# First k rows on ScalarE's DMA queue, v rows ahead of the weights, and the first masks as a bias product on TensorE

## The chip, the cores and the metric

The kernel runs on one core of one Trainium2 chip. The metric is the device time of one execution in microseconds (us). A profiled execution also has a span, from the first instruction to the last, which is about 1.7 us shorter than its time. Every time is a median of 3 to 6 runs, and the interval of its ratio to the kernel before is given with it.

The engines are called by their short names in the profile: PE is TensorE's matmuls, PEld its weight loads, DVE VectorE, ACT ScalarE, POOL GpSimd and SP SyncE.

## The reference

Sliding-window attention with four sink keys feeds a small mixture of experts in which every expert sees every token. B, H, S, D = 4, 8, 768, 64; window 128; 3072 tokens of 512 features; 4 experts with a hidden size of 1024.

```python
scores = scale * np.matmul(q, k.transpose(0, 1, 3, 2))
keep   = is_sink | in_window          # key < 4, or 0 <= query - key < 128
scores = np.where(keep, scores, -1e9)
a      = softmax(scores)
x      = np.matmul(a, v)              # heads put side by side: 3072 x 512
p      = domain_probs / (domain_probs.sum(-1, keepdims=True) + 1e-09)
for e in range(4):
    out += p[:, e:e+1] * (np.maximum(x @ w1[e], 0) @ w2[e])
```

## The kernel before

The sequence of each of the four batches is cut into three groups of 256 tokens. Attention of the first groups of batch 0 comes first; expert products start as soon as the first rows of x exist and from then on hide the attention of everything that follows. So the start is the only place where TensorE has too little to do. It is filled with idle products (matmuls of zeros, put there to keep the granted clock up; it is 1.00 in the windows below).

The order in which instructions are put on each engine is made at build time by a small model: `t[...]` are modelled engine times, `landed[...]` modelled arrivals of loads, and `later(engine, ready, slack, run)` puts an instruction in when the model thinks it is ready. Constants such as 4700.0 below are such modelled nanoseconds. They change the order of instructions and nothing else.

Loads go out on two kinds of queues. `nc.sync` and `nc.scalar` are plain queues, issued from SP and ACT. `nc.gpsimd` is the software queue: POOL spends about 0.9 us on each issue, one load after the other.

```python
def load_first():                       # q and k rows of the first group, two halves
    for half in range(2):
        for name, src in (("q", q), ("k", k)):
            nc.sync.dma_start(out=raw[name][:, half], in_=...)     # cut
        landed["first", half] = ((4700.0, 4700.0), (7000.0, 7900.0))[half]
        t["sp"] += 1060

# ... cut: the program's order at the start
load_v(0, (0, 1))                       # POOL: v0, v1
# POOL: two affine selects make the identity
for tb in (2, 3):
    load_nat(0, tb)                     # POOL: q, k rows of the second group (4 loads, tile qkn)
load_w1(0, 2)                           # POOL: first expert's w1 in two halves
# DVE: identity, then six instructions that make mask0 and mask1
cast_first(0)                           # ACT casts k, DVE casts q (first half)
# POOL: two affine selects make the selector sel2
cast_first(1)
load_v(0, (2, 3))                       # POOL: v2, v3
load_w2(0)

def scores(b, hp, g):                   # one pair of heads, one group
    # ... TensorE: 6 products into sps ; ACT: exp into a
    # batch 0: DVE multiplies each half of a by mask0 or mask1
```

The softmax here doesn't subtract the row's maximum and nothing guards it: scores larger than these inputs give would overflow.

Of the kernel before, what the change touches and what calls it, by code (L numbers as in the profile page):

```python
# [16 lines left out]
def kernel(  # L17
# [12 lines left out]
    nc = tc.nc  # L30
# [29 lines left out]
    NGATE = 5  # L60
    START = {0: 1, 1: 2}
    ONACT = 1
    FAST = tuple(START)
    UNITS = ("P1", "P5", "P6", "P2", "P7", "P3", "P4")
    DX = D + 1
# [1 line left out]



    t = {"pe": 1200.0, "act": 0.0, "dve": 0.0, "pool": 420.0, "sp": 800.0, "sw": 4700.0, "hw": 0.0}  # L70
    ring, whole = [0.0] * 6, [False] * 6
    WARM = 6600.0
    FLIP, LATE = 300, 2500
# [40 lines left out]
    def later(engine, ready, slack, run):  # L114

        pend.append((ready, ready + slack, engine, run))
# [89 lines left out]
    def load_first():  # L206

        raw = {name: mo.tile([P, 2, 4, 2 * D], FP32, name=f"{name}raw", tag=f"wide{i}", bufs=1) for i, name in enumerate("qk")}
        for half in range(2):
            hs = slice(4 * half, 4 * half + 4)  # L210
            for name, src in (("q", q), ("k", k)):
                x = raw[name][:, half]
                nc.sync.dma_start(
                    out=x, in_=src[0, hs, 0:G, :].rearrange("h (p t) d -> p h (t d)", t=2),
                )
                nat[0, half, name, "raw"] = x
            landed["first", half] = ((4700.0, 4700.0), (7000.0, 7900.0))[half]
            t["sp"] += 1060

    def copy(engine, out, in_):  # L220
        (nc.scalar.copy if engine == "act" else nc.vector.tensor_copy)(out=out, in_=in_)
# [168 lines left out]

    held = consts.tile([P, 2], BF16, name="held")
    nc.vector.memset(identf, 1.0)
    zeros = wpool.tile([P, 2 * G], BF16, name="zeros", tag=f"wf_{E - 2}")
    nc.vector.memset(zeros, 0.0)
    vsf = consts.tile([P, B, DX], FP32, name="vsf")
    nc.vector.memset(vsf, 0.0)
# [1 line left out]
    for h in range(H):  # L398
# [1 line left out]
        nc.sync.dma_start(  # L400
            out=vsf[r:r + NSINK, :, 0:D], in_=v[:, h, 0:NSINK, :].rearrange("b j d -> j b d"),
        )
    load_v(0, (0, 1))
    ident = consts.tile([P, P], BF16, name="ident")
    for sgn in (1, -1):
        nc.gpsimd.affine_select(
# [1 line left out]
            base=0, pattern=[[sgn, P]], channel_multiplier=-sgn,  # L408
        )
        pool(0, fixed=320)  # L410
    for tb in (2, 3):
        load_nat(0, tb)
    load_w1(0, 2)

    for x in vx:
        nc.vector.memset(x[:, :, D:DX], 1.0)
    nc.vector.tensor_copy(out=ident, in_=identf)
    mask0 = consts.tile([P, 3 * P], BF16, name="mask0")
    mask1 = consts.tile([P, 4 * P], BF16, name="mask1")
    nc.vector.tensor_tensor_scan(mask0[:, 0:P], ident, ident, 0.0, ALU.add, ALU.max)  # L420
    own = mask0[:, 0:P]
    prev = mask0[:, P:2 * P]
    nc.vector.tensor_scalar(out=prev, in0=own, scalar1=-1.0, scalar2=1.0, op0=ALU.mult, op1=ALU.add)
    for i, x in enumerate((prev, own)):
        nc.vector.tensor_copy(
            out=mask1.rearrange("p (n c q) -> p n c q", n=2, c=2)[:, :, i], in_=x[:, None, :].to_broadcast([P, 2, P]),
        )
    nc.vector.tensor_copy(out=mask0[:, 2 * P:3 * P], in_=own)
    nc.vector.memset(mask0[0:NSINK, 0:2 * P], 1.0)
    t["dve"] = 4600.0  # L430
    cast_first(0)
    flush(4700.0)

    sel2 = consts.tile([P, NHP, 2, DX], BF16, name="sel2")
    vsd = {}
    half = consts.tile([P, 2], BF16, name="half")
    ksd = [consts.tile([P, NHP, 32], BF16, name=f"ksd{i}") for i in range(2)]

    nc.vector.memset(sel2, 1.0)
    for base, sgn in ((0, 1), (NSINK - 1, -1)):  # L440
        nc.gpsimd.affine_select(
            out=sel2, in_=sel2, compare_op=ALU.is_ge, fill=0.0, base=base,
            pattern=[[-32 * sgn, NHP], [-NSINK * sgn, 2], [0, DX]], channel_multiplier=sgn,
        )
        pool(0, fixed=700)
    nc.vector.memset(half, 0.0)
    for ph in range(2):
        nc.vector.memset(half[64 * ph:64 * ph + 64, ph:ph + 1], 1.0)
    for x in ksd:
        nc.vector.memset(x, 0.0)  # L450
    t["dve"] += 900.0
    cast_first(1)
    load_v(0, (2, 3))
    load_w2(0)

    acc = [psum.tile([P, 2 * G], FP32, name=f"acc{i}", tag=f"o{i}", bufs=1) for i in range(2)]

# [104 lines left out]
    def scores(b, hp, g):  # L562
        T = qkT[b]
        w = sum(x[2] for x in GROUPS[g]) * P
        ready = scores_ready(b, hp, g)
        slots, sps = [], []
        for ph in range(2):
            i = pick()
            slots.append(i)
            sps.append(bank(i, [P, 2 * G], FP32, "sps"))  # L570
            ring[i] = 1e12
        c = 0
        for (kb, qb, nq) in GROUPS[g]:
            for ph in range(2):
                pr = slice(64 * ph, 64 * ph + 64)
                nc.tensor.matmul(  # L576
                    sps[ph][:, c:c + nq * P],
                    lhsT=T[pr, 1, hp, kb * P:(kb + 1) * P],
                    rhs=T[pr, 0, hp, qb * P:(qb + nq) * P],
                    start=True, stop=True,  # L580
                )
            c += nq * P
        scored_at[b] = done = pe(w, ready, n=6, switch=2)
        a = sb.tile([P, 2, w], BF16, name="aT", tag="aT", bufs=4)
        m = mask0 if g == 0 else mask1

        def masked(at):
            aT_at[b, hp, g] = at

        if b == 0:  # L590
            part = join(2, masked)
        else:
            def mask_both(at):
                def run(engine):
                    nc.vector.tensor_mul(a, a, m[:, None, :].to_broadcast([P, 2, w]))  # L595
                    masked(dve(2 * w, rate=1.92))
                later("dve", at, 1500, run)
            part = join(2, mask_both)
        for ph in range(2):
            def run(engine, ph=ph):  # L600
                nc.scalar.activation(out=a[:, ph], in_=sps[ph][:, 0:w], func=AF.Exp, scale=scale)  # L601
                at = act(w)
                take(slots[ph], at)
                if b:
                    part(at)
                    return

                def mask_one(engine):
                    nc.vector.tensor_mul(a[:, ph], a[:, ph], m)
                    part(dve(w, rate=1.92))  # L610
                later("dve", at, 300, mask_one)
            later("act", done, 300 + 10 * ph, run)
        aTs[b, hp, g] = a
# [101 lines left out]
    class Attention:  # L715
# [23 lines left out]
        def options(self):  # L739

            if self.valued:
                yield turn_ready(*self.valued[0]), "turn"
            if self.scored and len(self.valued) < 3:
                yield values_ready(*self.scored[0]), "values"
            if self.todo:
                kind, b, x, y = self.todo[0]
                if kind == "scores":
                    if len(self.scored) < 3:
                        yield scores_ready(b, x, y), "todo"
                elif kind == "keys":  # L750
                    yield max(turned(b, 0)), "todo"
                elif kind == "sinks":
                    yield max([free_at(), keys_at.get(b, 1e12)] + turned(b, x)), "todo"
            if self.flips:
                yield self.flip_ready() + (FLIP if self.b == 0 and self.flips[0][2] else 0), "flip"
# [620 lines left out]
```

## Time and profile before

| | before |
|---|---|
| time, median of 3 runs | 379.82 us (379.15 to 380.06) |
| PE busy, share of the span | 97% |
| idle products, all before 18 us | 7.42 us |
| first transpose (its weight load) starts | 6.51 us |
| scores of the second group start | 16.49 us |
| first expert product starts | 17.80 us |

The page's first part gives busy time and share of the span for each engine:

```profile
PE 367.0 (97%) x3954; PEld 298.7 (79%) x3954; DVE 271.8 (72%) x619; ACT 146.6 (39%) x383; POOL 71.6 (19%) x91
```

TensorE is full, but part of that is filler. The windows view of the idle products alone (window, its length, PE busy with the number of products, PEld busy, granted clock, DMA share, GB/s) shows where:

```profile
0.00:10.00 10.00, 5.66 (x20) 2.25 (x20) 1.00 1.23 162
10.00:14.00 4.00, 0.83 (x3) 0.29 (x3) 1.00 1.80 183
14.00:18.00 4.00, 0.93 (x7) 0.64 (x7) 1.00 1.50 195
...
```

The timeline of the start (start, busy time, engine, line, operation, out<-in, count, and in brackets the idle time before with what ended it) shows why the first transpose comes at 6.51 us:

```profile
4.72 0.62 ACT L221 CAST qkn<-kraw 128x512 bf16<-128x512 f32 x1 [2.64 <-DMA kraw<-in_k_dram]
...
4.96 0.80 DVE L425 COPY mask<-mask 128x256 bf16<-128x256 bf16 x2
...
6.10 0.35 DVE L221 CAST qkn<-qraw 128x512 bf16<-128x512 f32 x1
...
6.51 0.62 PE L479 MATMUL tr<-ident,qkn 128*128 128x128 bf16 x8 [0.87 <-DVE qkn L221]
```

The k rows are in at 4.7 us and cast at once. The q rows are in too, but VectorE is still copying masks, and the cast waits for it until 6.10.

A little later, the timeline of TensorE alone:

```profile
13.52 0.68 PE L479 MATMUL tr<-ident,qkn 128*128 128x128 bf16 x9 [0.47 <-DMA qkn<-in_k_dram]
...
14.55 0.93 PE L461 MATMUL acc<-zeros 128*128 128x256 bf16 x7
...
16.50 0.40 PE L576 MATMUL sps<-qkT 64*128 64x128 bf16 x6
...
17.80 1.05 PE L932 MATMUL hps<-xT,w 128*128 128x256 bf16 x8
```

The transposes of the second group wait for their rows (`qkn<-in_k_dram`); its scores follow 3 us later, and the first expert product (`hps`) right after them. The last of those rows was issued by POOL at 6.93 us. The answer for that one load gives its time to landing, so it landed at about 13.5 us:

```profile
L185 POOL DMA_DIRECT2D qkn<-in_k_dram x1: 881/881/881, 6.9 to 6.9; - x1
...
DMA to landing us min/median/max: 6.5/6.5/6.5
```

Last, the chain of waits that ended last, from the start (start, duration, piece). It does not pass through attention at all, but through POOL's issues and two weight loads:

```profile
7.81 0.92 POOL w L262
8.73 10.42 DMA w<-in_moe_w_dram
...
21.17 14.80 DMA w<-in_moe_w_dram
...
36.01 1.05 PE hps L932 x8
```

### The profile page before, as it was taken

How to read it: one execution, taken by the hardware profiler on the slowest of the kernel's cores; microseconds unless marked ns; L12 is line 12 of the kernel's file. 1: busy time of each engine (PE TensorE's matmuls, PEld its weight loads, DVE VectorE, ACT ScalarE, POOL GpSimd, SP SyncE). 2: the span in 40 equal slices, each digit the busy share in tenths (PEclk: the TensorE clock that was granted, in tenths of full speed). 3: DMA queues.
4: the chain of work that ended last, by engine and by line, in shares of the span. 5: the costliest groups of instructions: out<-in, count | busy, mean ns of one | idle time of the engine just before them, and what ended most of it. 6: DMA issues, size and time to landing. Idle time of an engine off the chain costs nothing.

```text
span 377.8 us, 9452 instructions
## 1 busy us (share of the span) xinstructions
PE 367.0 (97%) x3954; PEld 298.7 (79%) x3954; DVE 271.8 (72%) x619; ACT 146.6 (39%) x383; POOL 71.6 (19%) x91
## 2 busy tenths in 40 slices
PE   6889999999999999999999999999999999999995
PEld 3667667666666788888888888889999999999984
DVE  6774987755346898686598499489589496795780
ACT  4747433865555145436415446452112011111110
POOL 8954115601822092010110000000000000000000
PEclk9999999999999999999999999999999999999999
DMA  9999999930998999216394310122021111210101
GB/s 162 185 183 205 210 210 169 143 44 1 149 192 155 194 135 143 71 31 70 76 164 113 51 63 30 28 80 62 2 85 29 53 35 29 71 29 2 57 1 57
DMA packets 110807, 35.61 MB, mean 94 GB/s; under 512 B 94260, under 2 KB 106132, under 8 KB 110764
## 3 DMA queue, kind: packets, MB, share of 16 engines
q0 software_dynamic: 77520, 17.31, 50.8%
q1 hardware_dynamic: 33244, 17.70, 20.7%
q8 instruction: 31, 0.51, 0.5%
q14 instruction: 12, 0.10, 0.1%
HBM read 40.45 MB, written 6.34 MB: 124 GB/s over the span
## 4 chain that ended last, share of the span: by engine, by line
PE 87%; DMA 7%; POOL 2%; ACT 2%; issue 1%; DVE 1%; POOLq 0%; ACTq 0%; DVEq 0%
PE acc L1149 29%; PE hps L932 29%; PE cps L1009 12%; PE acc L1219 10%; DMA w<-in_moe_w_dram 7%; PE sps L576 3%; PE od L641 2%; POOL qkn L185 1%; POOL vx L250 1%; PE od L634 1%; ACT onat L680 1%; PE tr L479 1%; ACT aT L601 0%; PE sinks L546 0%; ACT osb L1182 0%
## 5 line engine op out<-in xcount | busy, mean ns | idle before, releaser
L932 PE MATMUL hps<-xT,w 128*128 128x256 bf16 x1056 | 131.4, 273 | 0.2
L932 PEld LDWEIGHTS <-w 128*128 128x128 bf16 x1056 | 99.3, 98 | 14.2 <-issue 1.6
L1149 PEld LDWEIGHTS <-H 128*128 128x128 bf16 x720 | 67.9, 98 | 11.2 <-issue 3.7
L601 ACT ACTIVATE aT<-sps 128x512 bf16<-128x512 f32 (+1 forms) x96 | 48.0, 567 | 34.1 <-PE sps L576 34.0
L956 DVE SCALAR_TENSOR_TENSOR H<-hps,gates 128x512 bf16<-128x512 f32 x84 | 57.0, 683 | 4.2 <-PE hps L932 3.6
L1149 PE MATMUL acc<-w,H 128*128 128x256 bf16 x432 | 56.4, 273 | 0.4 <-ACT acc L1173 0.4
L680 ACT ACTIVATE onat<-od,R 128x64 bf16<-128x64 f32 x144 | 33.2, 327 | 44.0 <-DVE R L668 43.9
L1219 PE MATMUL acc<-w,H 128*128 128x512 bf16 x192 | 45.4, 379 | 0.0
L250 POOL DMA_DIRECT2D vx<-in_v_dram x24 | 21.3, 895 | 83.2 <-PE od L641 70.9
L1149 PE MATMUL acc<-wf,H 128*128 128x256 bf16 x288 | 35.4, 273 | 0.8 <-ACT osb L1182 0.8
L595 DVE TENSOR_TENSOR aT<-aT,mask 128x1024 bf16<-128x1024 bf16 (+1 forms) x36 | 23.1, 641 | 16.7 <-ACT aT L601 16.5
L1182 ACT COPY osb<-acc 128x256 f32<-128x256 f32 x36 | 13.4, 373 | 55.0 <-PE acc L1149 54.9
L1219 PEld LDWEIGHTS <-H 128*128 128x128 bf16 x192 | 18.0, 98 | 18.3 <-issue 0.9
L1009 PEld LDWEIGHTS <-w 128*128 128x128 bf16 x480 | 30.6, 98 | 1.7 <-issue 0.8
L1028 DVE SCALAR_TENSOR_TENSOR H<-cps,gates 128x512 bf16<-128x512 f32 x45 | 30.6, 681 | 0.1
L1149 PEld LDWEIGHTS <-S 128*128 128x128 bf16 x288 | 27.7, 98 | 3.5 <-issue 0.3
L945 ACT ACTIVATE H<-hps 128x512 bf16<-128x512 f32 x35 | 21.3, 608 | 22.9 <-PE hps L932 22.9
L1037 ACT COPY cps<-cps 128x512 f32<-128x512 f32 x15 | 8.7, 582 | 44.1 <-PE cps L1009 44.1
L1009 PEld LDWEIGHTS <-vf 128*128 128x128 bf16 x360 | 22.5, 98 | 0.7 <-issue 0.2
L185 POOL DMA_DIRECT2D qkn<-in_k_dram x22 | 19.9, 907 | 10.4 <-DMA w<-in_moe_w_dram 8.5
L185 POOL DMA_DIRECT2D qkn<-in_q_dram x22 | 20.3, 922 | 8.6 <-DMA w<-in_moe_w_dram 7.5
L641 PE MATMUL od<-vx,aT 128*128 128x65 bf16 x352 | 20.4, 193 | 0.8 <-DMA vx<-in_v_dram 0.7
(92 smaller groups left out, 426.8 us busy)
## 6 DMA issues: line engine op xcount, KB each, us to landing
w<-in_moe_w_dram POOLq DMA_DIRECT2D x7, 1024.0 KB, 19.3
out_dram<-osb SPq DMA_DIRECT2D x24, 256.0 KB
gates<-gate_rows SPq DMA_DIRECT2D x36, 128.0 KB
vx<-in_v_dram POOLq DMA_DIRECT2D x24, 128.0 KB, 6.7
qkn<-in_q_dram POOLq DMA_DIRECT2D x22, 128.0 KB, 7.0
qkn<-in_k_dram POOLq DMA_DIRECT2D x22, 128.0 KB, 7.0
w<-in_moe_w_dram POOLq DMA_DIRECT2D x2, 512.0 KB, 9.3
qraw<-in_q_dram SPq DMA_DIRECT2D x2, 256.0 KB
```

Of the source, the lines that this page charges most:

```text
L185: nc.gpsimd.dma_start(out=both[:, i], in_=src[b, :, tb * P:(tb + 1) * P, :].rearrange("h p d -> p h d"),)
L250: nc.gpsimd.dma_start(out=vx[tb][:, :, 0:D], in_=v[b, :, tb * P:(tb + 1) * P, :].rearrange("h p d -> p h d"),)
L595: nc.vector.tensor_mul(a, a, m[:, None, :].to_broadcast([P, 2, w]))
L601: nc.scalar.activation(out=a[:, ph], in_=sps[ph][:, 0:w], func=AF.Exp, scale=scale)
L641: nc.tensor.matmul(od[:, qi, ph], lhsT=a[:, ph, c:c + P], rhs=vx[kb][:, 2 * hp + ph, 0:DX], start=(g == 0 and i == 0), stop=(i == len(term ...
L680: nc.scalar.mul(o[:, qi, hp, ph * D:(ph + 1) * D], od[:, qi, ph, 0:D], R[:, qi, ph])
L932: nc.tensor.matmul(h[:, i].rearrange("p (q n) -> p q n", q=2), lhsT=w1_sb[e][:, db, fb * P:(fb + 1) * P], rhs=xT[b, g][:, :, db], start=(i ...
L956: nc.vector.scalar_tensor_tensor(out=dst, in0=h, scalar=0.0, in1=gate, op0=ALU.max, op1=ALU.mult,)
L1009: nc.tensor.matmul(y[:, f], lhsT=A[:, d, f * P:(f + 1) * P], rhs=T[:, d], start=(m in ("P1", "P5") and f == 0 and d == 0), stop=(d == 1), ...
L1028: nc.vector.scalar_tensor_tensor(out=dst, in0=src, scalar=0.0, in1=gate, op0=ALU.max, op1=ALU.mult)
L1149: nc.tensor.matmul(x, lhsT=self.operand(b, g, e, m)[:, f], rhs=forms[e][m][:, f], start=(k == 0 and f == 0 and m in ("P1", "P5")), stop=(k ...
L1219: nc.tensor.matmul(op, lhsT=H[:, fb // QF, fb % QF, s], rhs=w2_sb[e][:, fb, :], start=(fb == 0), stop=(fb == NFB - 1),)
```

## The change

The intent: get the first group's plain rows in earlier and cast them at once, take the masks of the first group off VectorE, and have v rows there before they are waited for. The diff, cut to its core:

```diff
+    BIASED = 1
@@ load_first
-                nc.sync.dma_start(
+                (nc.sync if name == "q" else nc.scalar).dma_start(
@@ POOL's order at the start
-    load_v(0, (0, 1))
     # two affine selects: identity
+    # two affine selects: selector sel2 (was: after cast_first(0))
+    load_v(0, (0, 1))
     for tb in (2, 3):
         load_nat(0, tb)
+    load_v(0, (2, 3))
     load_w1(0, 2)
+    load_w2(0)
@@ masks: two tables of 0 and -32768, one half on DVE, one on ACT; mask0, mask1 later
-    # six DVE instructions that make mask0 and mask1, ahead of the casts
+    low = [lent[:, 5 * P:8 * P], lent[:, 8 * P:12 * P]]
+    ...
+        later("dve", 12000.0, 8000, run)      # make_mask: mask = low / 32768 + 1
@@ scores
+        biased = b == 0 and g < BIASED
+        if biased:
+            for ph in range(2):
+                nc.tensor.matmul(sps[ph][:, 0:w], lhsT=ident, rhs=low[min(g, 1)], start=True, stop=False, ...)
-                    start=True, stop=True,
+                    start=not biased, stop=True, skip_group_check=biased,
@@ after the exp
-                if b:
+                if b or biased:
                     part(at)
```

The modelled times were adapted with it, and one limit of the scheduler, `len(self.scored) < 3`, became 4 (both cut here). So the change also moves instructions on TensorE, VectorE and ScalarE.

More of the change, by code (lines that the diff above doesn't have):

```diff
@@ L66 @@
     DP = 72
-    t = {"pe": 1200.0, "act": 0.0, "dve": 0.0, "pool": 420.0, "sp": 800.0, "sw": 4700.0, "hw": 0.0}
+    t = {"pe": 1200.0, "act": 0.0, "dve": 0.0, "pool": 1280.0, "sp": 800.0, "sw": 6500.0, "hw": 0.0}
     ring, whole = [0.0] * 6, [False] * 6
@@ L216, in load_first @@
                 nat[0, half, name, "raw"] = x
-            landed["first", half] = ((4700.0, 4700.0), (7000.0, 7900.0))[half]
-            t["sp"] += 1060
+            landed["first", half] = ((4750.0, 4000.0), (6900.0, 5700.0))[half]
+            t["sp"] += 530
     def copy(engine, out, in_):
@@ L392 @@
     nc.vector.memset(identf, 1.0)
-    zeros = wpool.tile([P, 2 * G], BF16, name="zeros", tag=f"wf_{E - 2}")
+    lent = wpool.tile([P, 12 * P], BF16, name="lent", tag=f"wf_{E - 2}")
+    zeros = lent[:, 0:4 * P]
     nc.vector.memset(zeros, 0.0)
@@ L410 @@
         pool(0, fixed=320)
-    for tb in (2, 3):
-        load_nat(0, tb)
-    load_w1(0, 2)
-    for x in vx:
-        nc.vector.memset(x[:, :, D:DX], 1.0)
-    nc.vector.tensor_copy(out=ident, in_=identf)
-    mask0 = consts.tile([P, 3 * P], BF16, name="mask0")
-    mask1 = consts.tile([P, 4 * P], BF16, name="mask1")
-    nc.vector.tensor_tensor_scan(mask0[:, 0:P], ident, ident, 0.0, ALU.add, ALU.max)
-    own = mask0[:, 0:P]
-    prev = mask0[:, P:2 * P]
-    nc.vector.tensor_scalar(out=prev, in0=own, scalar1=-1.0, scalar2=1.0, op0=ALU.mult, op1=ALU.add)
-    for i, x in enumerate((prev, own)):
-        nc.vector.tensor_copy(
-            out=mask1.rearrange("p (n c q) -> p n c q", n=2, c=2)[:, :, i], in_=x[:, None, :].to_broadcast([P, 2, P]),
-        )
-    nc.vector.tensor_copy(out=mask0[:, 2 * P:3 * P], in_=own)
-    nc.vector.memset(mask0[0:NSINK, 0:2 * P], 1.0)
-    t["dve"] = 4600.0
-    cast_first(0)
-    flush(4700.0)
     sel2 = consts.tile([P, NHP, 2, DX], BF16, name="sel2")
-    vsd = {}
-    half = consts.tile([P, 2], BF16, name="half")
-    ksd = [consts.tile([P, NHP, 32], BF16, name=f"ksd{i}") for i in range(2)]
     nc.vector.memset(sel2, 1.0)
@@ L445, with make_mask, run @@
         pool(0, fixed=700)
+    load_v(0, (0, 1))
+    t["sw"] += 500
+    for tb in (2, 3):
+        load_nat(0, tb)
+    load_v(0, (2, 3))
+    load_w1(0, 2)
+    t["sw"] += 200
+    load_w2(0)
+    nc.vector.tensor_copy(out=ident, in_=identf)
+    own = lent[:, 4 * P:5 * P]
+    nc.vector.tensor_tensor_scan(own, ident, ident, 0.0, ALU.add, ALU.max)
+    two = own[:, None, :].to_broadcast([P, 2, P])
+    LOW = 32768.0
+    low = [lent[:, 5 * P:8 * P], lent[:, 8 * P:12 * P]]
+    nc.vector.tensor_scalar(
+        out=low[0].rearrange("p (n q) -> p n q", n=3)[:, 0::2], in0=two, scalar1=LOW, scalar2=-LOW, op0=ALU.mult, op1=ALU.add,
+    )
+    nc.vector.tensor_scalar(out=low[0][:, P:2 * P], in0=own, scalar1=-LOW, scalar2=None, op0=ALU.mult)
+    nc.vector.memset(low[0][0:NSINK, 0:2 * P], 0.0)
+    x = low[1].rearrange("p (n c q) -> p n c q", n=2, c=2)
+    nc.scalar.activation(out=x[:, :, 0], in_=two, func=AF.Copy, scale=-LOW)
+    nc.scalar.activation(out=x[:, :, 1], in_=two, func=AF.Copy, scale=LOW, bias=-LOW)
+    mask0 = consts.tile([P, 3 * P], BF16, name="mask0")
+    mask1 = consts.tile([P, 4 * P], BF16, name="mask1")
+    made = []
+    def make_mask(i):
+        def run(engine):
+            x = (mask0, mask1)[i]
+            nc.vector.tensor_scalar(out=x, in0=low[i], scalar1=1 / LOW, scalar2=1.0, op0=ALU.mult, op1=ALU.add)
+            dve(4 * P)
+            made.append(i)
+        later("dve", 12000.0, 8000, run)
+    for i in range(2):
+        make_mask(i)
+    t["dve"] = t["act"] = 4600.0
+    cast_first(0)
+    flush(4700.0)
+    for x in vx:
+        nc.vector.memset(x[:, :, D:DX], 1.0)
+    t["dve"] += 240.0
+    vsd = {}
+    half = consts.tile([P, 2], BF16, name="half")
+    ksd = [consts.tile([P, NHP, 32], BF16, name=f"ksd{i}") for i in range(2)]
     nc.vector.memset(half, 0.0)
@@ L450 @@
         nc.vector.memset(x, 0.0)
-    t["dve"] += 900.0
+    t["dve"] += 400.0
     cast_first(1)
-    load_v(0, (2, 3))
-    load_w2(0)
     acc = [psum.tile([P, 2 * G], FP32, name=f"acc{i}", tag=f"o{i}", bufs=1) for i in range(2)]
@@ L571, in scores @@
             ring[i] = 1e12
+        biased = b == 0 and g < BIASED
+        if biased:
+            for ph in range(2):
+                nc.tensor.matmul(sps[ph][:, 0:w], lhsT=ident, rhs=low[min(g, 1)], start=True, stop=False, skip_group_check=True)
+            pe(2 * w, ready, n=2)
         c = 0
@@ L603, in run @@
                 take(slots[ph], at)
-                if b:
+                if b or biased:
                     part(at)
                     return
+                assert len(made) == 2
                 def mask_one(engine):
@@ L747, in options @@
                 if kind == "scores":
-                    if len(self.scored) < 3:
+                    if len(self.scored) < 4:
                         yield scores_ready(b, x, y), "todo"
```

## The prediction

> **What bounds the kernel now.** TensorE. The page gives PE 97% busy of a 377.8 us span; the waits of PE after 36 us sum to only 1.7 us: nothing to gain there. What can be saved is PE time without useful work at the start. The windows view of PE's busy time shows about 5 us idle in the first 26 us. Idle products alone: 7.4 us of filler, all before 18 us. Together 12.6 us, 6.5 of it before the first transpose.
>
> **Why the first transpose is late (timeline).** The k rows are in at 4.72 (their cast on ACT starts), but VectorE is still making masks: the POOL selects for the identity come only at 3.31, behind two v loads of 0.9 us each, the mask work runs from 4.01 to 6.10, and the q cast waits for it. The first half therefore loses about 1.4 us. The second half is worse: once software-queue loads join, bytes fall from about 330 GB/s (plain loads alone, 3 us) to 100 to 240, and the second casts start at 8.02 and 8.94.
>
> **What the change does.**
> 1. k issues on ACT save about 1 us of issue (0.5 us each on SP). The skill's page "DMA: Bandwidth & Descriptors", section "Issuing engines are not separate DMA queues", says such a split saves only issue time; the larger part must come from step 2.
> 2. POOL makes identity and selector first (0.66 and 1.5 us), so software loads start near 3.7 instead of 1.31 us. The plain megabyte then runs almost alone: I estimate it is in by 6 to 7 us. The software loads lose little: estimated v0/v1 in at 8.5 to 9 (now 9.9 is waited for), rows of group 2 at 12.5 to 13 (now 13.5).
> 3. Masks are no longer in front of the cast: identity ready near 2.3, q cast at landing, first transpose near 5.2. Gain about 1.3 us.
> 4. Four head pairs get two bias products of 384 columns each: about 0.16 us each at the 2.4 columns per ns of the matmul spacing, 1.3 us in all, mostly inside filler. It removes eight VectorE multiplies of 0.35 us.
> 5. v2/v3 ahead of the weights: now waited for at 20.5 (0.53 us); estimated in by 15. The first weight half lands some 0.5 to 1 us later than its 16.0, the second near its 19.1, w2 near its 25.5 or slightly earlier.
>
> **Sum.** Attention of groups 1 and 2 is about 9.2 us of real PE work. If it is nearly all done when steady expert products begin near 17 to 17.5 us, PE has lost about 9 to 9.5 us instead of about 13 (12.6 plus 0.6 after 26 us). Gain 3 to 4 us; some is taken by the new limit, rows of group 2 at about 13 and the sink keys on POOL. Predicted 376.6 us (-0.85%), 8 in 10 within 374.8 to 378.9. Chances: faster by over 2% 0.02, within 2% 0.97, slower 0.01.
>
> **What would show it.** First transpose near 5.2; second casts before 7; no masks multiply in group 1; no PE wait for v at 20; idle plus filler near 9.5 us; PE after 40 us unchanged.
>
> **What would make it wrong.** Weights landing 2 us or more later, so that expert products start after 19 us; a different instruction order (the schedule is made from modelled times) that stalls PE later; v rows of group 1 as a new wait.

## More of the kernel before

Much later, the gate rows (p of the reference, one row of 256 tokens for each expert) are loaded on SP's queue as their five buffers come free:

```python
def load_gate(pair, e):
    x = mo.tile([P, 2, P], FP32, name="gates", tag="gates", bufs=NGATE)     # NGATE = 5
    nc.sync.dma_start(out=x..., in_=gate_rows[pair, e]...partition_broadcast(P))
    gate_sb[pair, e] = x
```

## The result, and the profile after

| | before | after |
|---|---|---|
| time, median of 4 runs each on the same chip | 379.75 us (379.15 to 380.06) | 380.01 us (379.21 to 380.44) |
| ratio after / before, 95% interval | | 1.0006 (0.9983 to 1.0029) |
| span, clock of the profiled run | 377.8 us, 1.0 | 377.9 us, 1.0 |
| first transpose (its weight load) | 6.51 us | 5.86 us |
| scores of the second group | 16.49 us | 16.63 us |
| first expert product | 17.80 us | 18.23 us |

376.6 us was predicted, and the measured median lies outside the range.

The page's first part and the idle products alone:

```profile
PE 367.5 (97%) x3953; PEld 299.4 (79%) x3966; DVE 270.5 (72%) x610; ACT 147.6 (39%) x386; POOL 71.1 (19%) x91
```

```profile
0.00:10.00 10.00, 5.16 (x14) 1.96 (x14) 1.00 1.28 164
10.00:14.00 4.00, 0.87 (x7) 0.63 (x8) 1.00 2.18 146
14.00:18.00 4.00, 1.98 (x15) 1.09 (x13) 1.00 1.23 191
...
```

There is not less filler but a little more: 5.16 + 0.87 + 1.98 = 8.01 us instead of 7.42, and it has moved to later, to 14 to 18 us. The bias products come on top; the same view of their line has 1.14 us before 10 us and 0.91 us from 10 to 14 us, 2.05 us in all.

The timeline of the start:

```profile
4.86 0.62 ACT L222 CAST qkn<-kraw 128x512 bf16<-128x512 f32 x1 [0.76 <-DMA kraw<-in_k_dram]
4.87 0.36 DVE L222 CAST qkn<-qraw 128x512 bf16<-128x512 f32 x1
...
6.07 1.02 PE L499 MATMUL tr<-ident,qkn 128*128 128x128 bf16 x8
...
6.94 0.62 ACT L222 CAST qkn<-kraw 128x512 bf16<-128x512 f32 x1 [1.45 <-DMA kraw<-in_k_dram]
```

This is nearly as intended: the first half's casts come at landing, and the second half's k rows are cast at 6.94 instead of 8.94 us. Only the second q cast is no earlier (8.20 against 8.02 us), because a copy that waits for ACT stands in front of it in VectorE's order. Now TensorE alone, from 13.5 us:

```profile
13.51 0.93 PE L481 MATMUL acc<-lent 128*128 128x256 bf16 x7
...
14.61 0.83 PE L499 MATMUL tr<-ident,qkn 128*128 128x128 bf16 x12
15.28 1.15 PE L481 MATMUL acc<-lent 128*128 128x256 bf16 x9
...
16.64 0.95 PE L601 MATMUL sps<-qkT 64*128 64x128 bf16 x18
17.52 0.39 PE L481 MATMUL acc<-lent 128*128 128x256 bf16 x2
18.23 0.61 PE L958 MATMUL hps<-xT,w 128*128 128x256 bf16 x4 [0.32 <-DMA w<-in_moe_w_dram]
```

The first group is done earlier, and 18 idle products fill the gaps in the second group's work: 7 before its transposes, 9 between these and its scores, while VectorE and ScalarE copy them, and 2 before the first weights. The second group's last rows were issued later, at 8.29 us, behind the selects and v0 and v1, and landed 5.1 us after that, at 13.35 us. That is only 0.12 us earlier than before, and its scores start about 3 us after this landing in both kernels (3.0 and 3.3 us):

```profile
L186 POOL DMA_DIRECT2D qkn<-in_k_dram x1: 923/923/923, 8.3 to 8.3; - x1
...
DMA to landing us min/median/max: 5.1/5.1/5.1
```

The chain of waits from the start:

```profile
3.16 0.69 POOL sel L415
3.85 1.86 POOL vx L251 x2
5.72 3.50 POOL qkn L186 x4
...
11.63 10.16 DMA w<-in_moe_w_dram
21.84 1.05 PE hps L958 x8
```

It runs through POOL without a break: selector, v0 and v1, four row loads, v2 and v3, and then the second half of the first expert's w1, which lands at 21.79 us (19.14 before). TensorE waits for it.

### The profile page after: what moved, and what is told of

Its sections match the earlier page's. It is cut to its first block, busy times and chain, and to the rows that moved or that the text cites. A ratio compares the mean times of both kernels' runs of the same rounds, so it can differ in the third digit from the quotient of the medians.

```text
span 377.9 us, 9458 instructions
## 1 busy us (share of the span) xinstructions
PE 367.5 (97%) x3953; PEld 299.4 (79%) x3966; DVE 270.5 (72%) x610; ACT 147.6 (39%) x386; POOL 71.1 (19%) x91
## 4 chain that ended last, share of the span: by engine, by line
PE 91%; DMA 3%; POOL 2%; ACT 1%; issue 1%; DVE 1%; POOLq 0%; DVEq 0%
PE hps L958 30%; PE acc L1175 29%; PE cps L1035 12%; PE acc L1245 11%; PE sps L601 3%; DMA w<-in_moe_w_dram 3%; PE od L667 3%; POOL qkn L186 1%; POOL vx L251 1%; PE od L660 1%; PE tr L499 1%; ACT onat L706 1%; PE sinks L566 0%; POOL sel L415 0%; ACT qkT L222 0%
## 5 line engine op out<-in xcount | busy, mean ns | idle before, releaser
L1245 PE MATMUL acc<-w,H 128*128 128x512 bf16 x179 | 43.4, 379 | 1.0 <-issue 0.5
L1257 DVE SCALAR_TENSOR_TENSOR osb<-acc,scale_t,osb 128x512 f32<-128x512 f32 x18 | 13.5, 749 | 10.6 <-PE acc L1245 10.5
```

The source lines that it names most:

```text
L1245: nc.tensor.matmul(op, lhsT=H[:, fb // QF, fb % QF, s], rhs=w2_sb[e][:, fb, :], start=(fb == 0), stop=(fb == NFB - 1),)
```

## The experiments

Eighteen kernels ran, all correct, each with five rounds against the kernel before on the same chip. The expectations label theories by letters; here is what they are about, in words:

- Rows: the rows of the second group land no earlier, so what the first group gains becomes idle products.
- Weights: the selects or the v loads, now ahead of the weights on POOL, make the weights late.
- Order: an instruction in the wrong place (a cast, the masks, the bias products) gives the gain back.
- Gate rows: whatever lead is left is lost near 203 us, where the fourth batch waits for gate rows.

To follow a lead through the kernel I read the start of the same expert product in each trace: the 65th second-layer product (near 60 us), the 601st first-layer product (near 190 us) and the 1001st (near 351 us). Positive numbers are us ahead of the kernel before, each from one profiled run:

| kernel | near 60 us | near 190 us | near 351 us |
|---|---|---|---|
| after | 0.61 | 0.35 | -0.08 |
| k_on_act | 0.91 | 1.01 | -0.28 |
| best1 | 1.11 | 0.96 | 0.02 |
| before_g4 | -0.71 | -0.65 | -0.22 |
| kact_g4 | 0.93 | 0.88 | 1.32 |
| after_g4 | -0.09 | -0.23 | 0.20 |
| best_g4 | 1.76 | 1.62 | 2.05 |
| rows_first | 2.82 | 2.67 | 3.67 |
| best_rows | 2.23 | 2.07 | 3.07 |

In the first three rows a lead that was there at 190 us is gone at the end. That is one half of the answer; the size of the lead is the other.

One profile carries only so far. Four kernels, the change among them, have the change's start and differ only in later gate loads; they stand at 0.61 (after), -0.09, -0.50 and -0.18 us near 60 us; the four that start like k_on_act stand at 0.64 to 0.93. So the change's lead of 0.61 us is within the spread of its own start, and that of k_on_act holds in all four of its profiles. In rows_first and best_rows the instruction order differs too, so the same product there does not mean the same work done.

### One part undone: the v rows, the cast, the bias

**v_behind** puts v2 and v3 back behind the first expert's w1.

```diff
-    load_v(0, (2, 3))
     load_w1(0, 2)
+    load_v(0, (2, 3))
```

> The changed kernel, with the v rows of the second group issued behind the first weights again (one part undone). Theory A (the software queue's stream sets when steady expert products begin): first weights land near 16.2 and 19.9 us instead of 18.18 and 21.79, the first expert product starts near 17 us instead of 18.23, the total falls by 0.5 to 1.5 us below the changed kernel's. Theory B (the early order on ACT and PE loses the gain): first scores stay at 8.3 us and the total stays within 0.4 us.

Measured: 381.37 us, ratio 1.003 (1.0013 to 1.0048), a higher median than the change's own, though the intervals overlap. The w1 halves landed at 17.70 and 20.30 us instead of 18.18 and 21.79, w2 as before the edit (27.01). So in these two profiles v ahead of the weights costs the weights 0.5 to 1.5 us, and the time is not better without it. The edit also moved TensorE's instructions from about 17 us on, through the modelled arrivals, so it is not the v rows alone. The profiled run also had a stretch at half clock. The windows view of PE (busy, count, granted clock, DMA share, GB/s) shows it:

```profile
6.00:10.00 4.00, 1.74 (x18) 0.84 2.13 142
10.00:14.00 4.00, 3.86 (x40) 0.73 1.70 161
```

The clock record is at 0.5 for 3.4 us, from 8.8 to 12.2. The Trainium skill's page "TensorE: Matmul & The Clock Gate", Part 1, says that the clock goes to half when TensorE is idle over a free-running window of 3413 ns, and that the moment varies from run to run. The length agrees. The idleness does not quite: TensorE was busy for 1.46 us of the 3.4 us before this stretch, and for 1.4 to 1.6 us before each of the others of this length. Such stretches fell into some profiled runs (v_behind, k_on_act, late_cast, before_g4, kact_g4, kact_gates and, twice as long, ident_first) and, between 7 and 378 us, not into those of before and after. The profile of before_g4, which starts as the kernel before does, was 0.71 us behind it near 60 us with such a stretch, so a single profile of the start is uncertain by about a microsecond.

**late_cast** corrects the modelled landing of the k rows, so that ACT copies the first transposes before it casts the second half (in the changed kernel it is the other way round, and the first scores start at 8.34 instead of 7.83 us).

```diff
-            landed["first", half] = ((4750.0, 4000.0), (6900.0, 5700.0))[half]
+            landed["first", half] = ((4750.0, 4850.0), (6900.0, 6950.0))[half]
```

> The changed kernel, with the modelled landing of the second halves of q and k set to 6.9 and 6.95 us, so that ACT copies the first transposes before it casts the second k half. Theory B: first scores near 7.2 us instead of 8.34, total 0.5 to 1 us below the changed kernel's. Theory A: first scores move as in B, but the first weights still land at 18.2 us, the first expert product still starts near 18.2 us, and the total stays within 0.3 us.

Measured: 380.22 us, ratio 1.0011 (0.9992 to 1.003). No gain: TensorE then waited 1.8 us for the first weight half (19.23 us in that run). Moving the cast alone gains nothing.

**no_bias** keeps everything but the bias products; the masks are made early again and multiplied on VectorE.

```diff
-    BIASED = 1
+    BIASED = 0
-        later("dve", 12000.0, 8000, run)
+        later("dve", 4000.0, 0, run)
```

> The changed kernel with masks multiplied on VectorE in group 1 again (no bias products). Theory C (the eight bias products, 1.3 us of PE, took the gain): total 1 to 1.3 us below the changed kernel's. Theory A: their place is taken by idle products or waits, the first expert product starts at 18.2 us as before, total within 0.3 us.

Measured: 381.07 us, ratio 1.0026 (1.0 to 1.0051). No harm of the bias products, 2.05 us of TensorE, shows. They take the place of idle time (3.57 us up to 40 us with them, 5.56 without) and not of filler (8.01 and 7.69). Whether they help by the 1 us between the medians can't be said from these runs: the interval of no_bias overlaps that of the change.

### One part alone: k on ScalarE's queue, the identity first

**k_on_act** is the kernel before with the k rows on ACT's queue and nothing else.

```diff
-                nc.sync.dma_start(
+                (nc.sync if name == "q" else nc.scalar).dma_start(
```

> The kernel before with only the k rows moved to ACT's queue. If a second issuing queue saves only issue time: all four plain loads land within 0.5 us of the kernel before (last at 8.83), and the total is the same within 0.3 us. If the split itself gave the early landing of the changed kernel (last at 6.91): last landing before 7.5 us.

Measured: 379.54 us, ratio 0.999 (0.9976 to 1.0003). Two things follow. First, the last plain rows landed at 6.99 us instead of 8.83, with POOL's order unchanged. The issue of that load moved from 2.41 to 1.32 us, so 1.09 us are issue time, and the other 0.75 us are more than that. The software queue paid: its first packet came at 5.82 us instead of 3.69, though its first load was issued at 1.31 in both. Step 1 of the prediction leaned on the Trainium skill's page "DMA: Bandwidth & Descriptors", section "Issuing engines are not separate DMA queues", which says that a split only saves issue time. Here it also moved the turns: with two plain queues loaded, the software queue got nothing until the plain rows were nearly in. All 18 kernels with k rows on ACT agree: their last plain rows land at 6.85 to 7.49 us and their first software packet comes at 5.61 to 5.99; the two without (before, before_g4) have 8.83 and 9.30, 3.69 and 3.91. Second, this kernel leads by 1.01 us at 190 us and has lost it all at 221 us. The wait of PE near there in the kernel before, then those of PE and of DVE in this one, in three answers:

```profile
PE sps L576 <- ACT onat L680: 0.5, 1, 0.5
```

```profile
PE sps L576 <- ACT onat L680: 1.8, 1, 1.8
```

```profile
DVE H L956 <- DMA gates<-gate_rows: 1.7, 1, 1.7
```

TensorE waits for attention outputs, ACT for VectorE, and VectorE for gate rows. SP's queue at this time:

```profile
186.30 11.15 SPq L197 DMA_TRANSPOSE qkT<-qkn  x5
...
199.56 1.97 SPq L384 DMA_DIRECT2D gates<-gate_rows  x4
```

Four gate loads stand behind the transposes of the last batch, which hold the queue for 11 us; issuing one of the five takes 4.35 us of them. The first of the four goes out at 198.99 us in the kernel before, 199.15 after the change and 199.56 here. It does not come earlier when TensorE does. So it acts as a deadline: the kernel before meets it with a wait of 0.5 us, the change with 0.9, this one with 1.8.

**ident_first** is k_on_act with POOL's identity selects ahead of the loads and corrected modelled landings: step 3 of the prediction with the masks still ahead of the cast, only made earlier, and without bias products. The order on TensorE, VectorE and ScalarE changes with the modelled landings.

```diff
-    load_v(0, (0, 1))
     # identity selects on POOL
+    load_v(0, (0, 1))
```

> The kernel before with k rows on ACT's queue, identity selects first on POOL (selector and v of group 2 stay behind, no bias products), modelled landings corrected. Theory: the first transpose comes near 5.3 us instead of 6.51, and the weights land no later than in k_on_act (15.4, 18.0, 24.9 us) plus 0.7 us; at 60 us the lead over the kernel before is 1 to 2 us, but the end is the same within 0.5 us, as near 203 us the lead is swallowed. Rival (an earlier first transpose is worth nothing because rows of group 2 and weights gate): the lead at 60 us is 0.9 us or less, as k_on_act.

Measured: 382.38 us, ratio 1.0063 (1.0041 to 1.0084), the slowest of all. The first expert product started at 16.91 us, the earliest of all, but in the profiled run two windows at half clock followed (24.9 to 31.7 us), and it was 2.81 us behind near 60 us. Half of these 6.8 us, about 3.4, is my estimate of what they cost, so they would account for nearly all of it. The timed runs are slow as well, and the record gives each of the six a mean clock below 1 (0.989 to 0.996); but k_on_act has 0.994 or 0.995 in four of its five runs without being slow, so where the stretch falls would have to matter. That was not tested, and the run says nothing against or for the other theories.

### The weights and the masks

**sel_behind** moves the selector's memset and its two selects on POOL behind the loads.

```diff
-    sel2 = consts.tile(...)       # memset on DVE, two affine selects on POOL
     load_v(0, (0, 1))
     # ... rows, v2, v3, weights
+    sel2 = consts.tile(...)       # now just before cast_first(1)
```

> The changed kernel, with only the selector's two selects on POOL put back behind the first loads. If POOL's later first load is what delays the weights (first at 18.2, second at 21.8, w2 at 27.0 us against 16.0, 19.1, 25.5 before): all three land 0.7 to 1.5 us earlier than in the changed kernel. If the v rows ahead of them or the engines' sharing is the cause: within 0.4 us of the changed kernel. In both cases the total moves less than 0.8 us while the wait near 203 us stays.

Measured: 379.37 us, ratio 0.9997 (0.9976 to 1.0017). The weights landed earlier: 16.88 and 19.90 us instead of 18.18 and 21.79, w2 at 25.32 instead of 27.04. So the two selects, 1.48 us at the head of POOL's order, do reach the weights. Other traces say the same: the first half lands at 16.86 to 16.94 us in the four kernels with the selects behind, and at 18.18 to 19.70 in the seven that keep the change's order of loads on POOL; rows_first, with the selects in front and 16.91 us, is the exception. But the interval contains the change's own ratio, so what the weights alone are worth is not resolved.

**mask_early** makes the masks for the later groups at once instead of near 13 us, where they fell together with POOL's work. In the changed kernel's timeline, VectorE and POOL there:

```profile
13.24 0.25 DVE L450 TENSOR_SCALAR mask<-lent 128x384 bf16<-128x384 bf16 x1
...
13.96 1.30 DVE L450 TENSOR_SCALAR mask<-lent 128x512 bf16<-128x512 bf16 x1
```

```profile
13.99 1.12 POOL L544 TENSOR_TENSOR vsd<-vsf,sel 128x520 bf16<-128x520 f32 x1
```

A third more columns took 1.30 instead of 0.25 us while POOL multiplied (the same instruction took 0.28 us in v_behind, after POOL's multiplication), and a copy of the second group's transposes came after it, at 15.38 us. The Trainium skill's page "SBUF — State Buffer", section "Terms", describes a port pair that VectorE and GpSimd lock for a whole instruction, so that the other one blocks. These two records agree with it: the mask ends 0.15 us after POOL's multiplication does. Which of the two had the lock first they don't show; VectorE's record starts 0.03 us earlier, and starts on POOL are rough.

```diff
-        later("dve", 12000.0, 8000, run)
+        later("dve", 5000.0, 0, run)
```

> The changed kernel with the two mask tiles made on VectorE near 5 us, where it idles, not at 13 to 15 us. Theory E (making them beside POOL's multiplication, one of them for 1.3 us instead of 0.25, holds up the copies of group 2's transposes): group 2's scores start near 15.8 us instead of 16.63. Theory A: the first expert product still waits for its weights near 18.2 us, the total stays within 0.4 us. Rival: the total falls by 0.8 us.

Measured: 379.77 us, ratio 0.9999 (0.9987 to 1.0012). The second group's scores started at 16.06 instead of 16.63 us, and the total did not move: TensorE then waited 1.2 us for the first weights.

### Gate rows: two misses, then the right loads

I first moved the wrong loads. **after_gates** and **kact_gates** issue the gate rows of the last batch on POOL, **after_gates8** and **kact_gates8** those of one more pair, so 12 and 16 of the 36 loads.

```diff
-        nc.sync.dma_start(
+        (nc.gpsimd if pair >= 3 * NG else nc.sync).dma_start(     # gates8: 3 * NG - 1
```

> The changed kernel, with the twelve gate loads of the fourth batch issued on POOL instead of SP; order on PE, DVE and ACT unchanged. Theory D (a lead gained early is swallowed near 203 us, where gate rows come late from SP's queue behind six transposing loads): the PE wait of 0.9 us on ACT onat near 204 us disappears, and the total falls by 0.4 to 0.9 us against the changed kernel. Rival (the wait at 204 us comes from DVE or ACT work): wait and total unchanged.

> The kernel before with k rows on ACT's queue and the fourth batch's gate loads on POOL. Theory D: the lead of about 0.9 us which the k rows on ACT had at 60 and 190 us is kept to the end; the 1.8 us wait near 203 us disappears; total 1.0 to 1.5 us below the kernel before, 0.6 to 1.2 us below k_on_act. Rival: the lead is lost again near 203 us, total as k_on_act.

> The changed kernel with the same sixteen gate loads on POOL. Theory D: the PE wait of 0.9 us near 204 us is gone; total 0.4 to 0.9 us below the changed kernel, so 0.3 to 0.8 us below the kernel before. Rival: unchanged.

> As kact_gates, but with the gate loads that were really waited for (the last third of batch 2 too, sixteen loads) on POOL; order on PE, DVE and ACT unchanged. Theory D: VectorE's wait of 1.7 to 1.9 us for gate rows near 203 us is gone, PE's wait of 1.8 to 2.0 us there too, and the lead of 0.9 us at 60 us lasts to the end: total 1.0 to 1.5 us below the kernel before. Rival (the load is late whatever queue issues it, as the engines are busy with transposing loads): wait stays above 1 us, total as k_on_act.

Measured: 380.82 (ratio 1.0024), 380.86 (1.0028), 380.45 (1.0013) and 379.37 us (0.9995). The wait near 203 us stayed: 0.8, 2.0, 1.2 and 1.5 us, and in kact_gates 3.4 us at half clock came after it. The trace says why: the first gate load on POOL came at 232.5 us in kact_gates8, and the four at 200 to 202 us were still on SP. Counted from the first gate load, they are the 14th to 17th of 36. I had taken them for the last batch's from their time, without counting.

**best1** put together what had helped so far on the changed kernel: selector behind the loads, masks early, and those 16 gates.

> The changed kernel with the selector's selects behind the loads, masks made near 5 us, and sixteen gate loads on POOL. If these three are what took the gain: weights at 16.9, 19.9, 25.3 us, group 2's scores near 16 us, first expert product near 17.2 us, no wait near 203 us; total 1.5 to 2.5 us below the kernel before. If group 2's rows (landing near 13.5 us in every kernel so far) gate: lead at 60 us stays at or below 1 us, total 0.5 to 1 us below.

Measured: 379.19 us, ratio 0.998 (0.9967 to 0.9994): the first kernel below both, by 0.2%.

Then the right four loads, on four kernels, with the order of TensorE, VectorE and ScalarE unchanged:

```diff
-        nc.sync.dma_start(
+        (nc.gpsimd if 13 <= len(gate_sb) < 17 else nc.sync).dma_start(
```

> The kernel before with only the four gate loads that go out at 199.5 to 201.2 us on SyncE's queue (the 14th to 17th of the 36) moved to GpSimd's; three of them stand ahead of the v loads of the last batch there, one behind. Theory D (these gate rows, stuck behind six transposes, are what swallows a lead near 203 us): the gates are issued before 190 us, TensorE's wait for the output copies near 203 us (0.5 us here) goes to under 0.2, the time falls by 0.1 to 0.5 us: 379.3 to 379.7. Rival (the gates are only the last named wait; something else in the last batch is late as well): the wait keeps its size under another name, time as before within 0.1%.

> k rows on ScalarE's queue alone, plus the same four gate loads on GpSimd. This form has the largest loss near 203 us (a lead of 1.0 us at 190 us becomes -0.28 at 221). Theory D: the VectorE wait for gate rows (1.7 us) is gone, TensorE's wait for the output copies falls from 1.8 to under 0.6 us, the lead at 221 us is 0.6 to 1.2 us and the time 378.6 to 379.2. Rival: the lead is lost at another wait by 221 us, time 379.4 to 379.9.

> The changed kernel plus the same four gate loads on GpSimd. Theory D: the 0.4 us that it leads at 190 us stay, time 379.3 to 379.8. Rival: no change, 379.8 to 380.3.

> The changed kernel with the selector selects behind the loads and the masks made early, plus the same four gate loads on GpSimd (instead of the last 16 gates, which missed the ones that are waited for). Theory D: the lead of 1.0 us at 190 us stays: 378.5 to 379.0. Rival: 379.1 to 379.4, as without the right gates moved.

| | time | ratio to before (95%) | same form without this edit | PE's wait near 203 us, without and with it |
|---|---|---|---|---|
| before_g4 | 379.60 us | 0.9997 (0.9983 to 1.0012) | 1 | 0.5, none |
| kact_g4 | 378.46 us | 0.997 (0.9958 to 0.9983) | 0.999 | 1.8, none |
| after_g4 | 379.57 us | 0.9996 (0.9983 to 1.0008) | 1.0006 | 0.9, none |
| best_g4 | 378.38 us | 0.9964 (0.9951 to 0.9977) | 0.998 (with 16 other gates moved) | 1.4, none |

In kact_g4 the first of the four goes out ten microseconds earlier, now from POOL:

```profile
L384 POOL DMA_DIRECT2D gates<-gate_rows x1: 571/571/571, 189.6 to 189.6; - x1
```

The cleanest measure is the stretch between the 601st and the 701st first-layer product. It took 30.95 us before, 31.39 after the change, 32.24 in k_on_act and 31.89 in best1. With the edit it took 30.52, 30.52, 30.51 and 30.51. So the place of these four loads is shown to be what took the lead there. One effect isn't separated: without them on SP's queue the transposes ended earlier too, as the longest issue of one took 2.0 to 2.4 us in these four kernels and 3.1 to 4.4 us without the edit. It also shows what the kernel before loses there, 0.43 us, which the time of before_g4 doesn't resolve: its profiled run, with a stretch at half clock from 7.7 us, had fallen 0.7 us behind already by 60 us.

### The rows of the second group

The last two kernels swap four row loads and two v loads on POOL, and the modelled arrivals with them. **rows_first** does it on the changed kernel (with the masks early, since this order needs them, and the four gate loads on POOL); **best_rows** does it on best_g4. As the order on TensorE, VectorE and ScalarE is made from the modelled arrivals, it changes too: best_rows and best_g4 differ in it from about 11 to 280 us. So the two runs test the swap together with the order that comes with it.

```diff
-    load_v(0, (0, 1))
     t["sw"] += 500
     for tb in (2, 3):
         load_nat(0, tb)
+    load_v(0, (0, 1))
     load_v(0, (2, 3))
```

> The changed kernel with the four gate loads on GpSimd and the masks made early, and the rows of the second group ahead of v0 and v1 on the software queue. Theory A (the rows of the second group, landing at 13.35 us, set when its scores start, and that is why the first group's earlier work turned into idle products): without two v loads in front of them the rows land near 11.5 to 12, the second group's scores start near 14.5 to 15.2 (16.63 in the changed kernel) and there are fewer idle products at 14 to 18 us than 1.98 us. The total depends on whether v0 and v1, now behind the rows (near 13.4), delay the first group's values: about 14 and not before 10.3, so the first expert product may come no earlier; 378.8 to 379.6. Rival: the scores still start after 16.2 us, because the copies of the transposes, not the rows, set the time.

> The fastest version so far (378.38) with the rows of the second group ahead of v0 and v1. Theory A: second group's scores near 14.5 to 15.2 (15.99 there); the first expert product near 17 as there, as the weights land no earlier; 377.8 to 378.5. Rival: later values of the first group push the first expert product behind 18 us, 378.6 to 379.4.

Measured: rows_first 377.20 us (376.17 to 379.36), ratio 0.9941 (0.9907 to 0.9974). best_rows 376.64 us (376.37 to 376.81), ratio 0.9914 (0.9888 to 0.9941), the fastest of all and 0.9% below both kernels. The profiled run of rows_first happens to be the fastest of its six. TensorE's timeline there, from 12.3 us:

```profile
12.32 0.39 PE L499 MATMUL tr<-ident,qkn 128*128 128x128 bf16 x4
...
12.98 0.71 PE L667 MATMUL od<-vx,aT 128*128 128x65 bf16 x18
...
14.29 0.40 PE L601 MATMUL sps<-qkT 64*128 64x128 bf16 x6
...
17.45 1.05 PE L958 MATMUL hps<-xT,w 128*128 128x256 bf16 x8
```

The second group's scores start at 14.29 instead of 16.63 us, and the idle products between 14 and 18 us are gone. Values of the first group (`od<-vx,aT`) now stand between the second group's transposes and its scores, where the change had idle products. The last rows landed at 11.03 us instead of 13.35:

```profile
L186 POOL DMA_DIRECT2D qkn<-in_k_dram x1: 896/896/896, 6.6 to 6.6; - x1
...
DMA to landing us min/median/max: 4.5/4.5/4.5
```

It is their place in the software queue that counts, not the time of issue: best_g4 issued its last rows at 6.35 us, 1.94 us before the change did, and they landed at 13.34. In the change, rows_first, best_g4 and best_rows the queue's first packet came at 5.65 to 5.79 us, and its 128 KB loads then landed 0.8 to 1.0 us apart on average; the last rows are sixth in line in the change and in best_g4, fourth in the other two.

The first group's values now come from 12.98 us on instead of 10.52, as v0 and v1 land later, and TensorE's waits up to 40 us show none for them. Nor did the first expert product have to come earlier: in best_rows it starts at 18.04 us, later than in best_g4 (17.28). But more of the attention is out of the way then: all 24 score products of the second group have run, in best_g4 18. The chain of waits of best_rows begins with the k rows and has no weight load in it any more:

```profile
1.32 6.17 DMA kraw<-in_k_dram
7.51 0.62 ACT qkn L222
```

One caution. rows_first also had its weights earlier than the change, at 16.91 and 20.03 us, with the same issue times, so part of its gain may be that. best_rows against best_g4 is free of that, though not of the changed order: there the weights landed at 16.9 us in both (the second halves at 19.7 and 19.4), and the rows at 11.31 instead of 13.34. The medians differ by 378.38 - 376.64 = 1.74 us, in two batches on two chips. The two profiled runs differ by 1.02 us, of which the table of leads has 0.47 near 60 us and the rest after 190 us. So how much of the gain is the rows' landing and how much the new order is not separated.

## Why the prediction was wrong

**What was right.** TensorE was the bound, and the start the place. The first casts came at landing, the second halves landed before 7 us (though one of their casts came at 8.20), the first transpose came at 5.86 us (5.2 was predicted), no mask multiply was left in the first group, and no wait for v at 20 us. The bias products took 2.05 us (1.3 estimated), in the place of idle time.

**The step that failed** is the one headed "Sum": "If it is nearly all done when steady expert products begin near 17 to 17.5 us, PE has lost about 9 to 9.5 us instead of about 13", with the new limit of "rows of group 2 at about 13" entered only as "some is taken". The condition was not met, and the limit took nearly everything. Counting idle time, idle products and bias products up to 40 us (length of the window less PE's busy time, plus filler and bias), the kernel before lost 5.60 + 7.42 = 13.0 us and the change 3.57 + 8.01 + 2.05 = 13.6 us. A few matmul records can be missing, so this is good to perhaps a microsecond, but not to the 4 us that were expected. The second group's scores start about 3 us after its last rows land, and these landed at 13.35 instead of 13.47 us. So the time that the first group's faster work set free went to idle products. The estimate for these rows was even about right (12.5 to 13); what was missing was to ask what TensorE would do until then. In best_rows the same count gives 2.62 + 7.09 + 1.95 = 11.7 us.

**Two terms were mis-sized.** The weights came 2.2, 2.65 and 1.6 us later (w1 in two halves, w2) where 0.5 to 1, about 0 and about 0 were estimated; step 2 counted the selects on POOL, but step 5 carried little of them on to the weights. The prediction did name late weights, with expert products after 19 us, as what would make it wrong. In the profile of the change these started at 18.23 us; in the three others with the same start (after_g4, after_gates, after_gates8) the first half landed at 18.82 to 19.70 and they started at 19.15 to 19.74 us. So the late weights count for more than the one profile shows. sel_behind shows that the selects are part of it; rows_first, with the selects still in front and the first half at 16.91 us, shows that they need not delay the weights. Part of the second half's delay is in how far the 16 completion increments of one load spread: the second w1 half had its 15th at 20.5 and its last at 21.8 us in the change, 19.4 and 20.0 in rows_first. What sets this spread is open. And step 1 credited the split with issue time alone, where it brought 1.84 us.

**One statement was wrong in what it implied.** "The waits of PE after 36 us sum to only 1.7 us: nothing to gain there." There was little to gain, but one of these waits, 0.5 us near 203 us, is for a load that goes out at a nearly fixed time. Any lead makes it longer. It took 0.4 us from the change and 1.3 us from k_on_act, so probably no version of this change could have shown its full lead at the end while the gate rows stood where they did (argued from the four runs above and not shown; rows_first was not run without that edit).

**The account**, from ratios times 379.7 us. The change stands at +0.2 us. Selector behind the loads and masks early, with 16 gate loads that were not the ones waited for, bring it to -0.8 (best1), the right four gate loads to -1.4 (best_g4), the rows, with the order that comes with them, to -3.3 (best_rows). A gain of the predicted 3 to 4 us did exist, with edits that the prediction didn't contain; the change as it was written reached none of it.

**What stays open.** What the longest transpose on SP's queue waits for, so that the queue gets free at nearly the same time whatever TensorE's lead; what sets the spread of the increments; why ident_first is slow; what the rows' landing is worth without the new order; and whether the kernel before would gain from the order of the rows alone, which was not run.

## What to carry to other kernels

When work at the start is made faster, follow the chain of waits to the next input that does not move, and move that one in the same change: here two v loads of 128 KB stood in front of the rows that the whole start waited for, and swapping them, with the instruction order that came with it, was worth more than all the rest. A small wait late in a full kernel can be a deadline; look for what it waits for and whether that comes earlier when everything else does. And count which of a row of identical loads is the one waited for before moving any.

## What the Trainium skill lacked or had wrong

- "DMA: Bandwidth & Descriptors", section "Issuing engines are not separate DMA queues": it says that issuing from several engines only saves sequencer time. In k_on_act the last plain rows landed 1.84 us earlier (8.83 to 6.99) for 1.09 us of issue saved, and the software queue's first packet came 2.1 us later (3.69 to 5.82).
- The same page, section "Queues, rings and completion order": it describes each engine as taking turns between queue rows, packet by packet. The runs show that with two plain queues loaded the software queue's first packet came 4.5 us after its first issue (2.4 us with one). Apart from taking turns, the page has nothing on which kind of queue goes first.
- The same page, section "Latency and other measured facts": it calls two of the DMA engines usually slower, without a figure. Here the last of a load's 16 increments came 0 to 1.5 us behind the 15th, and differently for the same load in different kernels; which engine it is was not looked up.
- No page of those read has what a queue of DMA transposes does to ordinary loads behind it. Five transposes held SP's queue for 11.15 us in k_on_act, and moving four gate loads out from behind them took 0.4 to 1.7 us off the stretch near 203 us.
